# Building fp32 weights from doubles by shifts and masks instead of exponent and mantissa arithmetic, in a fused convolution and SoLU layer

## The chip, the cores and the metric

The kernel runs on one core of a Trainium2 chip. A core has TensorE (PE, matrix products, with its weight loads shown as PEld), VectorE (DVE), ScalarE (ACT), GpSimd (POOL) and SyncE (SP, which issues the DMAs here). Each engine works its own instructions in order and waits for the others by semaphores. The metric is device time in microseconds.

## The reference

A causal convolution over seven taps, one set of softmaxed taps for each of 8 heads, is followed by a two-layer block with a SoLU and a layer norm between the products. Cut to what matters:

```python
# x (8, 4160, 192) f32; weight (8, 7); w_in (192, 1024) f64; w_out (1024, 192) f64; g_ln (1024,)
w = softmax(weight, axis=-1)                     # with 1e-9 in the denominator
x = causal_conv(x, w)                            # each head has 24 of the 192 columns
x = x.reshape(8 * 4160, 192)
h = x @ w_in
e = exp(h - max(h))
solu = h * e / (sum(e) + 1e-9)
mu, var = mean(solu), mean((solu - mu) ** 2)
ln = (solu - mu) / sqrt(var + 1e-6) * g_ln
out = (ln @ w_out).astype(float32)
```

w_in and w_out arrive as doubles, that is as pairs of 32-bit words, and the chip has no double. The kernel makes fp32 values of them itself.

## The kernel before, in words

The 33280 rows of x are 260 tiles of 128 rows. For each tile PE forms ph (128 x 1024) from the convolved input yT and the weights w_in; DVE takes the maximum (`emit_max`), ACT the exponential (`emit_exp`), DVE the product (`emit_mul`), ACT a half-precision copy (`emit_hi`), POOL the rest of it (`emit_lo`); a DMA transposes both, and PE forms the output tile po from them and w_out (`emit_out`). The convolution of the next chunk of rows is done on PE in between (`pc`). The order of the instructions on every engine is the order in which the code is written; nothing is rescheduled.

All weights are held as two halves in fp16, an upper part (whi for w_in, ohi for w_out) and a lower one (wlo, olo), after a scale by a power of two (t_in, t_out). All of that is prepared once at the start, while the first tiles already run. w_in has 192 rows: 128 of them fill A, in two halves of 512 columns (`halves[0]`, `halves[1]`), and the other 64 rows, folded to 128 x 512, are Z. w_out is W, 128 x 1536.

The class `Words` makes floats of the doubles: `exponents` and `mantissas` cut them out of the upper word on DVE, `join` adds the lower word, ACT turns the exponent bits into a power (`powers`), `signs` puts the sign in, and `value` multiplies. For W part of this runs on POOL (`lows`, `whole`, `value`) and on ACT (`floats`, and `out_powers`, which brings g_ln in). ACT's `squares` give the sums from which the scales t_in and t_out come. `settle` makes the lower halves of the first convolved rows and issues their transposes. `out_mean` takes the mean of w_out's columns on PE, `out_upper` subtracts it on DVE and makes ohi on ACT, `out_lower` makes olo on DVE. `first_two` and `second_two` are the code of the first four tiles, in which W's steps are mixed. In `second_two` the order on PE is: two tiles of ph, the first convolution of chunk 1 (`hold`), the sum for t_out, the mean, and then the next tiles.

PSUM holds three pairs of banks for ph and two single banks. A tile's pair comes free with its `emit_mul`; `hold` takes the pair of tile 1, and the sixth tile's ph the pair of the fourth.

Of the kernel before, what the change touches and what calls it, by code (L numbers as in the profile page):

```python
# [8 lines left out]
F16 = mybir.dt.float16  # L9
F32 = mybir.dt.float32  # L10
# [9 lines left out]
def kernel(  # L20
# [10 lines left out]
    P = 128  # L31
# [355 lines left out]
    for j in range(2):  # L387
# [10 lines left out]
    rebias = cp.tile([P, 1], F32, name="rebias")  # L398
    pool.memset(rebias, -916.0 * 2.0**23)
    act.activation(rebias[0:1], rebias[0:1], AF.Copy)  # L400
    mhalf = cp.tile([P, 1], F32, name="mhalf")
    pool.memset(mhalf, -0.5)
    band = cp.tile([TJ, H, TB, K], F32, name="band")
    pool.memset(band, 1.0)
# [14 lines left out]
    even = cp.tile([P, P], F32, name="even")  # L419
    pool.memset(even, 1.0 / F)  # L420
# [6 lines left out]
    class Words:  # L427


        def __init__(self, raw, name):  # L430
            self.name = name
            n = raw.shape[1]
            self.low, self.high = raw.bitcast(U32)[..., 0], raw[..., 1]
            self.n, self.e = n, None
# [4 lines left out]
        def exponents(self, c):  # L439
            if self.e is None:  # L440
                self.e, self.m = (
                    sp.tile(
                        [P, GMAX * D], I32, name=f"{q}_{self.name}", tag="g_raw", bufs=3
                    )[:, 0 : self.n]
                    for q in "em"
                )
            dve.tensor_scalar(
                self.e[:, c], self.high[:, c], 0x7FF00000, None, ALU.bitwise_and
            )

        def mantissas(self, c):
            dve.tensor_scalar(
                self.m[:, c], self.high[:, c], 0xFFFFF, 0x100000,
                ALU.bitwise_and, ALU.bitwise_or,
            )

        def lows(self, c, scale):
            pool.tensor_scalar(
                self.low[:, c].bitcast(F32), self.low[:, c], scale, 1.0,
                ALU.mult, ALU.mult,  # L460
            )

        def floats(self, c):
            act.copy(self.m[:, c].bitcast(F32), self.m[:, c])

        def squares(self, c, to):

            junk = sp.tile([P, F], F32, name=f"oj_{self.name}_{c.start}", tag="sq", bufs=1)
            junk = junk.bitcast(F16)[:, 0 : c.stop - c.start]
            act.activation(  # L470
                junk, self.e[:, c].bitcast(F32), AF.Square, scale=2.0**20, accum_out=to
            )

        def whole(self, c):
            pool.tensor_tensor(
                self.f[:, c], self.m[:, c].bitcast(F32),
                self.low[:, c].bitcast(F32), ALU.add,
            )

        def join(self, c):  # L480
            dve.scalar_tensor_tensor(
                self.f[:, c], self.low[:, c], 2.0**-32, self.m[:, c],
                ALU.mult, ALU.add,
            )

        def powers(self, c):
            act.activation(self.e[:, c], self.e[:, c], AF.Relu, bias=rebias, scale=8.0)

        def signs(self, c, to):
            dve.scalar_tensor_tensor(  # L490
                to[:, c], self.high[:, c], -(2**31), self.e[:, c],
                ALU.bitwise_and, ALU.bitwise_or,
            )

        def value(self, c, powers, eng):
            f = self.f[:, c]
            eng.tensor_tensor(f, f, powers[:, c].bitcast(F32), ALU.mult)

    wi, A, Z = Words(raw_in, "in"), slice(0, F), slice(F, 3 * F // 2)
    HF = F // 2  # L500
    halves = [slice(0, HF), slice(HF, F)]

    def words(c):
        wi.exponents(c)
        wi.mantissas(c)
        wi.join(c)

    def valued(c):

        wi.signs(c, wi.m)  # L510
        wi.value(c, wi.m, dve)
# [23 lines left out]

    words(halves[0])
    wi.powers(halves[0])
    valued(halves[0])
# [11 lines left out]

    tp = pair(0, "tps")
# [16 lines left out]
    words(halves[1])  # L568
    for h in c0.halves(1):
        c0.sum_squares(*h)  # L570
    wi.powers(halves[1])
# [15 lines left out]
    isq = cp.tile([P, 2], F32, name="isq")  # L587
# [15 lines left out]
    going = convolve(*spans0[0], [pq[:, 0:512], pq[:, 512:F]])  # L603
    got0 = [next(going)]
    c0.add_up()
    got0 += going
    wi.squares(A, isq[:, 0:1])
    wi.signs(halves[1], wi.m)
    wi.exponents(Z)
    wi.powers(Z)  # L610
    for f in chain0[1:-3]:
        f()
    wi.squares(Z, isq[:, 1:2])
    for pc, hg in got0:
        c0.upper(pc, *hg)
    wi.value(halves[1], wi.m, dve)
    wi.mantissas(Z)
    c0.open(0, None)
    got1 = got0
    wo, W = Words(raw_out, "out"), slice(0, NFC * D)  # L620

    tp = total(isq, "wi")
    got0 = list(convolve(*spans0[1], [single("pr_0"), single("pr_1")]))
    dve.tensor_reduce(isq[:, 0:1], tp, AX.X, ALU.add)
    for f in root_power(t_in, isq[:, 0:1], 2.0**26, 1e-12):
        f()
    for c in halves:
        act.activation(whi[:, 0, c], wi.f[:, c], AF.Copy, scale=t_in)
# [44 lines left out]
    gate = cp.tile([1, 1], F32, name="gate")  # L673
    o_inv = cp.tile([P, 1], F32, name="o_inv")
    t_out = cp.tile([P, 1], F32, name="t_out")
    osq = cp.tile([P, 1], F32, name="osq")
    wof = wo.f.rearrange("p (c d) -> p c d", d=D)
    mean = None

    def out_powers():  # L680


        woe = wo.e.bitcast(F32).rearrange("p (c d) -> p c d", d=D)
        for j in range(NFC):
# [23 lines left out]
    def out_upper():  # L708
        for c in quarters:
            dve.scalar_tensor_tensor(  # L710
                wof[:, c], wof[:, c], 1.0,
                mean[:, 0:D].unsqueeze(1).broadcast_to([P, NFC // 2, D]),
                ALU.mult, ALU.subtract,
            )
            act.activation(ohi[:, c, :], wof[:, c], AF.Copy, scale=t_out)
# [433 lines left out]
    def first_two():  # L1149
# [21 lines left out]
        wo.value(W, wo.e, pool)  # L1171
# [426 lines left out]
```

## Time and profile before

| | us |
|---|---|
| median of 3 timed runs | 1166.07 |
| lowest and highest | 1162.34, 1166.71 |
| span of the profiled execution, first to last instruction | 1161.5 |
| PE busy in it | 1132.2 |
| DVE busy in it | 1016.8 |
| ACT busy in it | 998.0 |
| POOL busy in it | 878.6 |

The profiled execution shows no other time of its own than its span, which lies 4.6 us under the median of the timed runs and 0.8 us under the lowest of them. Busy time is a sum over the whole span. What the start of the kernel costs has to be read from that stretch.

### The profile page before, as it was taken

The page shows a single profiled execution, that of the slowest core. Times are in us where ns is not written, and L with a number is a line of the kernel's source. Part 1 is how long each engine was busy: PE and PEld are TensorE (multiplying, and loading weights), DVE is VectorE, ACT ScalarE, POOL GpSimd, SP SyncE. Part 2 cuts the span into 40 slices and gives each one's busy share as a digit, 9 for nine tenths or more (in the row PEclk, how much of TensorE's full clock was granted, in tenths as well). Part 3 has the DMA queues.
Part 4 walks back from the last instruction along what each step waited for, and adds up shares of the span by engine and source line. Part 5 has one row for each costly group of instructions (what it writes and reads, how often), then busy time and mean ns, then how long its engine had stood idle before and what let it go on. Part 6 is the DMA issues. An engine that isn't in the chain of part 4 may idle for free.

```text
span 1161.5 us, 22374 instructions
## 1 busy us (share of the span) xinstructions
PE 1132.2 (97%) x7742; PEld 692.4 (60%) x7742; DVE 1016.8 (88%) x2058; ACT 998.0 (86%) x1775; POOL 878.6 (76%) x686
## 2 busy tenths in 40 slices
PE   5898999999999999999999999999999999999998
PEld 3575566656666665655656666665666566566556
DVE  8888898988989898998889989888898988788787
ACT  6998988888888888888888888898888889888886
POOL 2745879987888588887868888588788858855665
PEclk9999999999999999999999999999999999999999
DMA  8799899999999999999999999999999998999988
GB/s 226 171 181 180 185 218 205 205 201 202 200 213 195 195 186 220 207 189 199 202 198 190 208 209 199 187 202 208 206 204 198 195 193 170 174 177 186 181 163 188
DMA packets 727391, 226.95 MB, mean 195 GB/s; under 512 B 651614, under 2 KB 725870, under 8 KB 727278
## 3 DMA queue, kind: packets, MB, share of 16 engines
q1 hardware_dynamic: 727278, 225.53, 100.2%
q8 instruction: 60, 0.98, 0.3%
q14 instruction: 53, 0.43, 0.1%
HBM read 33.00 MB, written 25.56 MB: 50 GB/s over the span
## 4 chain that ended last, share of the span: by engine, by line
PE 88%; DVE 5%; ACT 2%; DMA 2%; issue 2%; POOL 1%; SPq 0%; DVEq 0%; ACTq 0%; POOLq 0%
PE po L859 40%; PE ph L736 36%; PE pc L281 6%; PE ph L759 5%; DVE e L807 1%; DMA pT<-p 1%; DVE ph L790 1%; DMA raw_in<-in_moe_w_in_dram 1%; ACT e L797 1%; ACT sq L819 0%; DVE raw L869 0%; DVE y L322 0%; POOL p L827 0%; PE mean L701 0%; DVE wlo L647 0%
## 5 line engine op out<-in xcount | busy, mean ns | idle before, releaser
L827 POOL TENSOR_TENSOR p<-e,p 128x1024 f16<-128x1024 f32 x257 | 548.3, 2138 | 219.5 <-ACT p L815 218.0
L859 PE MATMUL po<-ohl,pT 128*128 128x192 f16 (+1 forms) x4264 | 539.8, 283 | 7.8 <-DVE raw L869 5.4
L859 PEld LDWEIGHTS <-pT 128*128 128x128 f16 x4264 | 384.4, 98 | 167.1 <-issue 7.6
L736 PE MATMUL ph<-whi,yT 128*128 128x512 f16 x1548 | 419.1, 380 | 2.7 <-DVE e L807 2.6
L790 DVE TENSOR_SCALAR_CACHE_REDUCE ph<-ph,cv 128x1024 f32<-128x1024 f32 x248 | 319.1, 1288 | 72.9 <-PE ph L759 56.6
L797 ACT ACTIVATE e<-ph,sm 128x1024 f32<-128x1024 f32 x260 | 289.4, 1113 | 102.0 <-DVE ph L790 95.8
L807 DVE SCALAR_TENSOR_TENSOR e<-ph,cv,e 128x1024 f32<-128x1024 f32 x248 | 317.1, 1279 | 26.0 <-ACT e L797 25.7
L736 PEld LDWEIGHTS <-yT 128*128 128x128 f16 x2064 | 192.6, 98 | 231.3 <-issue 36.3
L815 ACT CAST p<-e 128x1024 f16<-128x1024 f32 x257 | 266.8, 1039 | 27.9 <-DVE e L807 27.3
L819 ACT ACTIVATE sq<-e 128x1024 f32<-128x1024 f32 x260 | 273.4, 1052 | 0.2
L736 PE MATMUL ph<-wlo,yT 128*128 128x512 f16 x516 | 153.5, 379 | 0.0
L869 DVE TENSOR_REDUCE raw<-po 128x192 f32<-128x384 f32 x247 | 136.3, 552 | 14.3 <-PE po L859 13.9
L243 POOL TENSOR_TENSOR xs<-xr,xs 128x960 f16<-128x960 f32 (+1 forms) x56 | 107.6, 1922 | 1.4
L313 ACT ACTIVATE y<-pc 112x432 f16<-112x432 f32 (+5 forms) x140 | 62.8, 469 | 13.8 <-PE pc L281 8.1
L759 PE MATMUL ph<-wlo,yT 64*128 64x512 f16 x269 | 74.0, 380 | 0.0
L322 DVE SCALAR_TENSOR_TENSOR y<-pc,y 112x432 f16<-112x432 f32 (+5 forms) x140 | 72.2, 532 | 0.8 <-ACT y L313 0.8
L281 PE MATMUL pc<-xs,taps_hi 128*112 128x240 f16 (+1 forms) x448 | 72.9, 261 | 0.0
L759 PE MATMUL ph<-wlo,y 64*128 64x512 f16 x251 | 68.6, 380 | 0.0
L181 DVE TENSOR_REDUCE xa<-xr 128x1 f32<-128x384 f32 x112 | 66.6, 617 | 0.0
L281 PEld LDWEIGHTS <-taps_hi 128*112 128x112 f16 x448 | 52.4, 130 | 16.4
L240 POOL TENSOR_SCALAR xr<-xr,s 128x960 f32<-128x960 f32 (+1 forms) x56 | 57.5, 1027 | 2.9
L281 PE MATMUL pc<-xs,taps_lo 128*112 128x240 f16 (+1 forms) x224 | 58.5, 261 | 0.0
(148 smaller groups left out, 787.6 us busy)
## 6 DMA issues: line engine op xcount, KB each, us to landing
out_dram<-raw SPq DMA_DIRECT2D x127, 192.0 KB, 3.0
xr<-in_x_dram SPq DMA_DIRECT2D x41, 480.0 KB, 4.7
xr<-in_x_dram SPq DMA_DIRECT2D x22, 384.0 KB, 4.1
pT<-p SPq DMA_TRANSPOSE x263, 4.6
y<-yT SPq DMA_DIRECT2D x15, 140.0 KB, 3.1
y<-yT SPq DMA_DIRECT2D x15, 126.0 KB, 3.1
yT<-y SPq DMA_TRANSPOSE x102, 3.7
raw_out<-in_moe_w_out_dram SPq DMA_DIRECT2D x1, 1536.0 KB
```

The lines of the kernel that those rows point to most:

```text
L243: (2.1 * size + 0.2, lambda: pool.tensor_tensor(xl, r, h, ALU.subtract)),
L281: nc.tensor.matmul(o, tp[:, h + j, :], r, start=q == 0, stop=q == len(ops) - 1)
L736: nc.tensor.matmul(bank, lhs, w[:, r, n * 512 : (n + 1) * 512], start=start and j == 0, stop=stop and j == len(ops) - 1,)
L759: nc.tensor.matmul(banks_of(t)[n], y[q, t.off : t.off + P], wlo[q, 1, n * 512 : (n + 1) * 512], start=start, stop=not start,)
L790: dve.tensor_scalar(t.ph, t.ph, t.cv[:, 0:1], None, ALU.mult, ALU.min, accum_out=t.bias)
L797: act.activation(t.e, t.ph, AF.Exp, bias=t.bias, scale=-1.0, accum_out=grp.z[:, g : g + 1])
L807: dve.scalar_tensor_tensor(t.e, t.ph, t.cv[:, 3:4], t.e, ALU.mult, ALU.mult, accum_out=t.grp.s1[:, t.g : t.g + 1],)
L815: act.copy(t.p16[:, :, 0, :], t.halves)
L819: act.activation(junk, t.e, AF.Square, accum_out=t.grp.s2[:, t.g : t.g + 1])
L827: eng.tensor_tensor(t.p16[:, :, 1, :], t.halves, t.p16[:, :, 0, :], ALU.subtract)
L859: nc.tensor.matmul(t.po[:, 0:n], t.pT[:, a, :], w, start=j == 0, stop=j == len(ops) - 1)
L869: dve.tensor_reduce(t.grp.raw[:, t.g, :], t.po[:, 0 : 2 * D].rearrange("p (a d) -> p d a", a=2), AX.X, ALU.add,)
```

## The change

`Words` now builds the float out of the double's bits. `sizes` takes the absolute value of the upper word (on DVE for the two halves of A, on ACT for Z and W), `bounded` raises it to at least 2^-15 (on DVE, with the largest value of each partition as a by-product, for w_in; on POOL for W), `shifted` shifts it by three bits and masks, `signs` puts sign and top exponent bit in, `lows` adds the top three bits of the lower word. Powers, joins and products go. The scale t_in comes from the largest value of each partition, rounded in the same way and summed over partitions by PE. g_ln no longer multiplies W on ACT: it is the weight of the product that makes the mean (`even`), and `out_upper` multiplies by it, in eight pieces of 192 columns instead of two of 768. The squares of W are taken from the float itself, scaled by the largest g_ln of the partition (`most`). The load of g_ln goes ahead of the load of w_out, and that load now waits for a one-element copy on POOL, which waits for the second part of w_in. The diff, cut to its core:

```diff
-    nc.sync.dma_start(
-        raw_out.rearrange("p (c d) t -> p c (d t)", d=D),
-        w_out.rearrange("(c p) d -> p c d", p=P),
-    )
+    nc.sync.dma_start(gl, g_ln.rearrange("(c p) -> p c", p=P))
...
-    pool.memset(band, 1.0)
+    dve.memset(band, 1.0)
...
-    even = cp.tile([P, P], F32, name="even")
-    pool.memset(even, 1.0 / F)
+    pool.tensor_copy(raw_out[0:1, 0, 0:1], raw_in[0:1, F - 1, 0:1])
+    nc.sync.dma_start(
+        raw_out.rearrange("p (c d) t -> p c (d t)", d=D),
+        w_out.rearrange("(c p) d -> p c d", p=P),
+    )
...
+        def sizes(self, c, eng):
+            if eng is act:
+                act.activation(self.m[:, c], self.high[:, c].bitcast(F32), AF.Abs)
+            else:
+                dve.tensor_scalar(
+                    self.m[:, c].bitcast(U32), self.high[:, c], 0x7FFFFFFF, None,
+                    ALU.bitwise_and,
+                )
+        def bounded(self, c, peak=None):
+            m = self.m[:, c]
+            if peak is None:
+                pool.tensor_scalar(m, m, LEAST, 1.0, ALU.max, ALU.mult)
+            else:
+                dve.tensor_scalar(m, m, LEAST, None, ALU.max, ALU.max, accum_out=peak)
+        def shifted(self, c):
             dve.tensor_scalar(
...
+                self.bits[:, c], self.m[:, c].bitcast(U32), 3, 0x3FFFFFF8,
+                ALU.logical_shift_left, ALU.bitwise_and,
+            )
+        def signs(self, c):
+            dve.scalar_tensor_tensor(
+                self.bits[:, c], self.high[:, c], 0xC0000000, self.bits[:, c],
                 ALU.bitwise_and, ALU.bitwise_or,
             )
...
+        def lows(self, c):
             dve.scalar_tensor_tensor(
...
+                self.bits[:, c], self.low[:, c], 29, self.bits[:, c],
+                ALU.logical_shift_right, ALU.bitwise_or,
+            )
...
+    wi.sizes(halves[0], dve)
+    wi.bounded(halves[0], peaks[:, 0:1])
     words(halves[0])
-    wi.powers(halves[0])
-    valued(halves[0])
...
-    words(halves[1])
-    for h in c0.halves(1):
-        c0.sum_squares(*h)
-    wi.powers(halves[1])
+    wi.sizes(halves[1], dve)
+    wi.bounded(halves[1], peaks[:, 1:2])
+    wi.sizes(Z, act)
...
+    act.activation(whi[:, 0, halves[0]], wi.f[:, halves[0]], AF.Copy, scale=t_in)
     settle(*spans0[0], got1)
+    wi.signs(halves[1])
+    wi.lows(halves[1])
+    act.activation(whi[:, 0, halves[1]], wi.f[:, halves[1]], AF.Copy, scale=t_in)
     for j in range(chunks[1].np):
         chunks[1].load(j)
-    nc.sync.dma_start(gl, g_ln.rearrange("(c p) -> p c", p=P))
-    wo.lows(W, 2.0**-32)
-    wi.join(Z)
-    valued(Z)
+    wo.sizes(W, act)
+    wo.bounded(W)
+    words(Z)
...
-    wo.exponents(W)
+    wo.shifted(W)
     for f in chain0[-3:]:
         f()
-    wo.mantissas(W)
...
-    wo.powers(W)
-    wo.floats(W)
...
                 start=(c == 0), stop=(c == NFC - 1),
...
     def out_upper():
-        for c in quarters:
-            dve.scalar_tensor_tensor(
-                wof[:, c], wof[:, c], 1.0,
-                mean[:, 0:D].unsqueeze(1).broadcast_to([P, NFC // 2, D]),
-                ALU.mult, ALU.subtract,
-            )
-            act.activation(ohi[:, c, :], wof[:, c], AF.Copy, scale=t_out)
+        for q in quarters:
+            for c in range(q.start, q.stop):
+                dve.scalar_tensor_tensor(
+                    wof[:, c], wof[:, c], gl[:, c : c + 1], mean[:, 0:D],
+                    ALU.mult, ALU.subtract,
+                )
+            act.activation(ohi[:, q, :], wof[:, q], AF.Copy, scale=t_out)
...
         emit_max(t)
         emit_exp(t)
-        wo.signs(W, wo.e)
-
-        pool.tensor_copy(gate, wo.e.bitcast(F32)[0:1, 0:1])
-        wo.whole(W)
+        wo.signs(W)
         emit_mul(t)
-        out_powers()
+        emit_hi(t)
         emit_max(u)
         emit_exp(u)
-        wo.squares(W, osq)
-        emit_hi(t)
+        wo.lows(W)
+        out_squares()
         settle_rest()
         emit_mul(u)
         emit_hi(u)
...
-        wo.value(W, wo.e, pool)
```

In the order of DVE's instructions the first place is that from the scale of chunk 0 (s) to the lower halves of w_in. Before, with e, m and f the exponents, the integer and the float of w_in, isq the sums of squares and y the convolved rows:

```order
L112 TENSOR_SCALAR s_167<-s_167 128x1
L497 TENSOR_TENSOR f_in<-f_in,m_in 128x512
L452 TENSOR_SCALAR m_in<-raw_in 128x512
L624 TENSOR_REDUCE isq<-pt_wi 128x1
...
L322 SCALAR_TENSOR_TENSOR y_0_0_192<-pq,s_167,y_0_0_192 112x5x64
L481 SCALAR_TENSOR_TENSOR f_in<-raw_in,m_in 128x512
L490 SCALAR_TENSOR_TENSOR m_in<-raw_in,e_in 128x512
L497 TENSOR_TENSOR f_in<-f_in,m_in 128x512
L647 SCALAR_TENSOR_TENSOR wlo<-f_in,t_in,whi 128x512 x2
```

Now, with m the sizes and peaks the largest of each partition:

```order
L112 TENSOR_SCALAR s_163<-s_163 128x1
L456 TENSOR_SCALAR m_in,peaks<-m_in 128x512
L588 TENSOR_SCALAR peak<-peaks 128x3
L591 SCALAR_TENSOR_TENSOR peak<-peaks,peak 128x3
L459 TENSOR_SCALAR f_in<-m_in 128x512
L596 TENSOR_REDUCE t_in<-pt_wi 128x1
...
L322 SCALAR_TENSOR_TENSOR y_0_0_181<-pq,s_163,y_0_0_181 112x5x64
L465 SCALAR_TENSOR_TENSOR f_in<-raw_in,f_in 128x512
L471 SCALAR_TENSOR_TENSOR f_in<-raw_in,f_in 128x512
L459 TENSOR_SCALAR f_in<-m_in 128x512
```

The second half of A got its float ahead of the scale; now its last two steps stand behind the three steps of `settle` (L322), ahead of Z's three.

On ACT the same stretch, from the upper halves of w_in's A to the first exponential, was this before (whi are the upper halves, those of 64x512 belong to Z; pr and y belong to the second half of the first convolved rows):

```order
L628 ACTIVATE whi<-f_in,t_in 128x512 x2
L313 ACTIVATE y_0_0_192<-pr_202,s_167 112x5x96
L313 ACTIVATE y_0_0_192<-pr_203,s_167 112x5x32
L313 ACTIVATE y_0_0_192<-pr_203,s_167 112x5x64
L644 ACTIVATE whi<-f_in,t_in 64x512 x4
L487 ACTIVATE e_out<-e_out,rebias 128x1536
L464 CAST m_out<-m_out 128x1536
L797 ACTIVATE e_297,z_268<-ph_273,sm_295 128x1024
```

The same stretch now:

```order
L605 ACTIVATE whi<-f_in,t_in 128x512
L609 ACTIVATE whi<-f_in,t_in 128x512
L443 ACTIVATE m_out<-raw_out 128x1536
L313 ACTIVATE y_0_0_181<-pr_198,s_163 112x5x96
L313 ACTIVATE y_0_0_181<-pr_199,s_163 112x5x32
L313 ACTIVATE y_0_0_181<-pr_199,s_163 112x5x64
L623 ACTIVATE whi<-f_in,t_in 64x512 x4
L776 ACTIVATE e_286,z_257<-ph_262,sm_284 128x1024
```

Two instructions over W behind Z's upper halves went, and one came ahead of them.

On DVE the next place is that of W's steps around the first two tiles, before (e_out is W's exponents, e_297 and e_313 the tiles'):

```order
L647 SCALAR_TENSOR_TENSOR wlo<-f_in,t_in,whi 64x512 x2
L447 TENSOR_SCALAR e_out<-raw_out 128x1536
L205 TENSOR_SCALAR cv_168<-s_167,t_in 128x1
L117 TENSOR_SCALAR cv_168<-cv_168 128x1
L452 TENSOR_SCALAR m_out<-raw_out 128x1536
L790 TENSOR_SCALAR ph_273,sm_295<-ph_273,cv_168 128x1024
L490 SCALAR_TENSOR_TENSOR e_out<-raw_out,e_out 128x1536
L807 SCALAR_TENSOR_TENSOR e_297,s_0_269<-ph_273,cv_168,e_297 128x1024
L790 TENSOR_SCALAR ph_274,sm_311<-ph_274,cv_168 128x1024
L322 SCALAR_TENSOR_TENSOR y_0_0_192<-pr_202,s_167,y_0_0_192 112x5x96
...
L807 SCALAR_TENSOR_TENSOR e_313,s_0_269<-ph_274,cv_168,e_313 128x1024
```

And now:

```order
L626 SCALAR_TENSOR_TENSOR wlo<-f_in,t_in,whi 64x512 x2
L459 TENSOR_SCALAR f_out<-m_out 128x1536
L205 TENSOR_SCALAR cv_164<-s_163,t_in 128x1
L117 TENSOR_SCALAR cv_164<-cv_164 128x1
L769 TENSOR_SCALAR ph_262,sm_284<-ph_262,cv_164 128x1024
L465 SCALAR_TENSOR_TENSOR f_out<-raw_out,f_out 128x1536
L786 SCALAR_TENSOR_TENSOR e_286,s_0_258<-ph_262,cv_164,e_286 128x1024
L769 TENSOR_SCALAR ph_263,sm_292<-ph_263,cv_164 128x1024
L471 SCALAR_TENSOR_TENSOR f_out<-raw_out,f_out 128x1536
L661 TENSOR_REDUCE most<-gl 128x1
L322 SCALAR_TENSOR_TENSOR y_0_0_181<-pr_198,s_163,y_0_0_181 112x5x96
...
L786 SCALAR_TENSOR_TENSOR e_294,s_0_258<-ph_263,cv_164,e_294 128x1024
```

One step over W's 1536 columns (L452) went from ahead of the first maximum, and one (L471) came between the second tile's maximum and its product, with a reduction of eight columns (L661). Behind the first four tiles every engine has the same instructions in the same order in both kernels.

## Rows read from the trace of the kernel before

**Rows 1.** The page: span and instructions.

```profile
span 1161.5 us, 22374 instructions
```

**Rows 2.** Busy us of each engine (instructions), granted PE clock, DMA, by stretches.

```profile
20.00:30.00 10.00, 6.88 (x27) 2.03 (x26) 9.75 (x14) 7.84 (x11) 2.40 (x5) 1.00 0.95 248
50.00:1161.50 1111.50, 1099.51 (x7556) 670.85 (x7554) 974.68 (x1976) 958.06 (x1703) 855.40 (x663) 1.00 1.01 195
```

**Rows 3.** The chain that ended last, 0 to 60 us: start, us, what.

```profile
32.72 1.76 issue
34.48 2.98 PE pc L281 x16
...
37.69 3.16 PE mean L701 x16
...
40.95 1.82 DVE f_out L710 x2
...
44.03 1.90 PE ph L736 x8
```

**Rows 4.** Timeline of ACT: start, us, instruction, idle time before it.

```profile
14.85 0.63 ACT L470 ACTIVATE oj_in<-e_in 128x512 f16<-128x512 f32 x1
15.48 1.34 ACT L313 ACTIVATE y<-pq,s 112x480 f16<-112x480 f32 x3
17.00 1.34 ACT L628 ACTIVATE whi<-f_in,t_in 128x512 f16<-128x512 f32 x2 [0.17 <-DVE t_in L112]
21.02 2.94 ACT L644 ACTIVATE whi<-f_in,t_in 64x512 f16<-64x512 f32 x4 [1.44 <-DVE f_in L497]
24.78 1.58 ACT L487 ACTIVATE e_out<-e_out,rebias 128x1536 int32<-128x1536 int32 x1 [0.81 <-DVE e_out L447]
```

**Rows 5.** Timeline of DVE, 11 to 20 us.

```profile
11.43 0.43 DVE L447 TENSOR_SCALAR e_in<-raw_in 128x512 int32<-128x512 int32 x1 [0.56 <-DMA raw_in<-in_moe_w_in_dram]
...
13.03 0.69 DVE L490 SCALAR_TENSOR_TENSOR m_in<-raw_in,e_in 128x512 int32<-128x512 int32 x1
13.64 0.42 DVE L447 TENSOR_SCALAR e_in<-raw_in 128x512 int32<-128x512 int32 x1
...
14.73 0.15 DVE L112 TENSOR_SCALAR s<-s 128x1 int32<-128x1 int32 x1
...
16.81 0.15 DVE L112 TENSOR_SCALAR t_in<-t_in 128x1 int32<-128x1 int32 x1
16.88 1.46 DVE L322 SCALAR_TENSOR_TENSOR y<-pq,s,y 112x480 f16<-112x480 f32 x3
```

**Rows 6.** Instructions of line L940, a DVE maximum with a by-product, 192 columns.

```profile
L940 DVE TENSOR_SCALAR_CACHE_REDUCE raw<-raw,t x128: 384/404/411, 96.4 to 1156.0; 128x192 f32<-128x192 f32 x128
```

**Rows 7.** Timeline of PE: the first convolution, in two parts, and the second.

```profile
10.63 1.94 PE L281 MATMUL pq<-xr,taps 128*112 128x120 f32 x8 [1.07 <-ACT taps L563]
...
15.87 1.87 PE L281 MATMUL pr<-xr,taps 128*112 128x120 f32 x16
```

**Rows 8.** Timeline of POOL: its first step over w_out.

```profile
17.42 1.59 POOL L458 TENSOR_SCALAR raw_out<-raw_out 128x1536 f32<-128x1536 uint32 x1 [12.56 <-DMA raw_out<-in_moe_w_out_dram]
```

**Rows 9.** Timeline of DVE, 23 to 37 us.

```profile
23.78 0.96 DVE L447 TENSOR_SCALAR e_out<-raw_out 128x1536 int32<-128x1536 int32 x1
...
25.84 1.30 DVE L790 TENSOR_SCALAR_CACHE_REDUCE ph<-ph,cv 128x1024 f32<-128x1024 f32 x1
...
27.04 1.77 DVE L490 SCALAR_TENSOR_TENSOR e_out<-raw_out,e_out 128x1536 int32<-128x1536 int32 x1
...
33.09 1.28 DVE L807 SCALAR_TENSOR_TENSOR e<-ph,cv,e 128x1024 f32<-128x1024 f32 x1 [0.28 <-ACT e L797]
```

**Rows 10.** DVE groups by form, 0 to 60 us: a product over 160 columns of PSUM.

```profile
L322 DVE SCALAR_TENSOR_TENSOR y<-pc,s,y 112x160 f16<-112x160 f32 x1 | 0.4, 375 | 0.0
```

**Rows 11.** By stretches, as rows 2: the granted PE clock behind the pause.

```profile
35.00:38.50 3.50, 3.50 (x19) 3.50 (x18) 2.63 (x9) 3.50 (x7) 3.50 (x3) 0.51 0.54 113
```

**Rows 12.** What PE waited for from 44 to 130 us: in total, times, longest.

```profile
PE po L859 <- DVE raw L869: 4.8, 4, 1.8
```

More of the change, by code (lines that the diff above doesn't have):

```diff
@@ L430, in __init__ @@
         def __init__(self, raw, name):
-            self.name = name
             n = raw.shape[1]
-            self.low, self.high = raw.bitcast(U32)[..., 0], raw[..., 1]
-            self.n, self.e = n, None
+            self.low, self.high = (raw.bitcast(U32)[..., j] for j in range(2))
+            self.m = sp.tile(
+                [P, GMAX * D], F32, name=f"m_{name}", tag="g_raw", bufs=3
+            )[:, 0:n]
             self.f = xp.tile(
@@ L437, in __init__ @@
             )[:, 0:n]
[L439 to L445, printed above, removed]
-                )
+            self.bits = self.f.bitcast(U32)
+        def sizes(self, c, eng):
[5 more added lines that the diff above has]
+                    ALU.bitwise_and,
+                )
@@ L466, in squares @@
[L466 to L471, printed above, removed]
-            )
[L474 to L478, printed above, removed]
@@ L501 @@
     halves = [slice(0, HF), slice(HF, F)]
+    peaks = cp.tile([P, 3], F32, name="peaks")
+    peak = cp.tile([P, 3], F32, name="peak")
     def words(c):
[L504 to L511, printed above, removed]
+        wi.shifted(c)
+        wi.signs(c)
+        wi.lows(c)
     wtop = cp.tile([TJ, H], F32, name="wtop")
@@ L549, in of_blocks @@
         return t[:, :, a * TB : z * TB].rearrange("p h (q c) -> p q h c", c=TB)
+    for h in c0.halves(1):
+        c0.sum_squares(*h)
     tp = pair(0, "tps")
@@ L602 @@
     pq = pair(1, "pq")
[L603 to L610, printed above, removed]
+    c0.add_up(single("pt_x0"))
+    got1 = list(convolve(*spans0[0], [pq[:, 0:512], pq[:, 512:F]]))
     for f in chain0[1:-3]:
         f()
-    wi.squares(Z, isq[:, 1:2])
-    for pc, hg in got0:
+    for pc, hg in got1:
         c0.upper(pc, *hg)
-    wi.value(halves[1], wi.m, dve)
-    wi.mantissas(Z)
+    wi.bounded(Z, peaks[:, 2:3])
+    pbits, kbits = peak.bitcast(U32), peaks.bitcast(U32)
+    dve.tensor_scalar(
+        pbits, kbits, 3, 0x3FFFFFF8, ALU.logical_shift_left, ALU.bitwise_and
+    )
+    dve.scalar_tensor_tensor(
+        pbits, kbits, 0xC0000000, pbits, ALU.bitwise_and, ALU.bitwise_or
+    )
+    tp = total(peak, "wi")
+    wi.shifted(halves[1])
+    dve.tensor_reduce(t_in, tp, AX.X, ALU.add)
+    dve.tensor_scalar(t_in, t_in, 1e-6, 2.0**-13, ALU.max, ALU.mult)
+    dve.tensor_scalar(
+        t_in.bitcast(I32), t_in.bitcast(I32), EXPO, None, ALU.bitwise_and
+    )
+    inverse_power(t_in, t_in, 1)
     c0.open(0, None)
-    got1 = got0
     wo, W = Words(raw_out, "out"), slice(0, NFC * D)
-    tp = total(isq, "wi")
     got0 = list(convolve(*spans0[1], [single("pr_0"), single("pr_1")]))
[L624 to L628, printed above, removed]
+    act.activation(whi[:, 0, halves[0]], wi.f[:, halves[0]], AF.Copy, scale=t_in)
     settle(*spans0[0], got1)
+    wi.signs(halves[1])
+    wi.lows(halves[1])
+    act.activation(whi[:, 0, halves[1]], wi.f[:, halves[1]], AF.Copy, scale=t_in)
     for j in range(chunks[1].np):
         chunks[1].load(j)
-    nc.sync.dma_start(gl, g_ln.rearrange("(c p) -> p c", p=P))
-    wo.lows(W, 2.0**-32)
-    wi.join(Z)
-    valued(Z)
+    wo.sizes(W, act)
+    wo.bounded(W)
+    words(Z)
     for pc, hg in got0:
```

52 lines of the change are left out of this document (14 added, 38 removed).

## The prediction

> **What bounds the kernel now.** The span is 1161.5 us [rows 1], and the stretches come next: from 50 us on PE is busy 1099.5 of 1111.5 us, while between 20 and 30 us it works only 6.9 of 10 and DVE works 9.75 [rows 2]. So the body is bound by PE, the start is not, and what delays PE's last long stop at the start is added to the end. The chain of waits says where that stop is [rows 3]: PE pauses 1.76 us ahead of the first convolution of chunk 1 (34.48), runs that and the mean, DVE subtracts the mean (40.95), and PE goes on at 44.03, from where its work is gapless for a long time. The timelines of ACT and DVE then tell what stands ahead of 34.48. Everything that the change touches lies ahead of 44.03, and behind the first four tiles the order is the same. I therefore carry times of single events from the trace into the new order and look at two of them: the start of the convolution (34.48) and PE's restart (44.03).
>
> **The change part by part.**
>
> *The scale t_in.* The second half of w_in lands at 11.43 [rows 5]. On it DVE now does sizes (0.43, as L447) and bounded. The trace has no maximum with a by-product over 512 columns: the same kind over 192 takes 0.40 [rows 6], and over 1024 columns of PSUM 1.30 [rows 9], so 1.08 ns a column between them and 0.40 + 320 x 1.08 ns = 0.75, which I take; below it lies L447's 0.43, above it two streams and a read of the by-product, 0.69 + 0.15. Then the five small steps to s (0.19 each, 0.15 and a gap): 13.6 instead of 14.88. ACT's sizes of Z (0.63 as L470, [rows 4]) start when Z is there, at 13.6 at the latest [rows 5]; bounded on DVE 14.2 to 15.0, two steps over three columns to 15.35. Before, it took 16.96 - 15.48 = 1.5 us from the end of the squares to t_in, with five small steps; now four are left: 1.3, so t_in is there at 16.6, some 0.35 earlier. The convolution now runs in one piece of 16 passes at the slow rate of that stretch (8 in 1.94, [rows 7]): 10.8 to 14.7, so ACT's first upper halves start at 14.7 instead of 15.48, ahead of t_in either way. Early on, then, a gain of 0.35.
>
> *Upper halves of w_in.* Before, both halves of A were ready at t_in and ACT rounded them at once (17.00 to 18.34). Now DVE first does the three steps of settle (1.46, to 18.05) and then signs and lows of the second half, 0.69 each by L490 [rows 5]: 19.45. Behind that wait on ACT stand: the second half's upper part (0.65), W's sizes (1.5, L487's 1.58 less what overlaps), the three upper halves of the second convolved part (1.34), and Z's four (2.94) [rows 4]. That gives 20.1, 21.6, 22.95 and 25.9, where Z's were done at 23.96 before: +1.9. PE needs them for the last four products of the first tile (0.24 each by rows 3, so 1.0): ph is there at 26.9.
>
> *W's load* is issued when the second part of w_in has landed: 11.43, a copy (0.2), an issue (0.6). Before, it landed at 17.42, 6.0 us behind that part [rows 8, 5], with Z's bytes still in front of it. So 18.2 if it takes the same 6.0 behind its issue. ACT takes it up at 20.1. The cover is thus 1.9 us, a third of the load's own time, and what is beyond it goes one for one into Z's upper halves. The load of g_ln costs nothing: only the convolved rows' transposes and W stand behind it.
>
> *W's steps on DVE.* The first maximum was at 25.84 behind DVE's own steps over W; now at 26.95, when ph is there: +1.1. Of the 1.9, the 0.8 is what the removed mantissas (of L447's kind and size, 0.96) leave free. Signs over 1536 columns stand behind it as before (L490's 1.77, [rows 9]). Between the second tile's maximum and its product lows is new: 1.77 by the same row, since it also reads two streams; at least 0.96, L447's time for one stream. I take 1.77, as two streams go at 1.05 ns a column (0.69 for 512, 1.77 for 1536) where one goes at half of that (0.43 and 0.96). The largest g_ln adds 0.15. DVE waited 0.28 for the exponential there [rows 9], which is now hidden. So the product of the second tile starts 1.1 + 1.77 + 0.15 - 0.28 - 0.1 = 2.6 later, at 35.7, and the convolution behind it on PE at 37.05.
>
> *From there to the mean* PE's work is the same 16 + 2 + 16 passes: 6.35 us from 34.48 to 40.85, 3.5 of it at half clock (granted 0.51, 1.2 GHz, [rows 11]) behind the pause. Taken over as it is: 43.4. What ACT and POOL lose (powers, g_ln, joins, products) was not waited for: POOL's float of W was there before PE came to the mean.
>
> *Subtracting the mean* in eight pieces of 192 columns instead of two of 768 (1.82 together, [rows 3]). A piece of 160 columns of PSUM takes 0.375 [rows 10]; back to back some 0.05 of it overlaps, so 0.33 to 0.40 each, 2.6 to 3.2: +0.8 to +1.4, taken as +0.9. The fourth tile's product stands behind it on DVE, and PE's restart behind that.
>
> *Sum:* 2.6 + 0.9 = +3.5 us. PE restarts at 47.5; the span becomes 1165.0, and on the median of the runs, which lies 4.6 above the span, 1169.6. The bounds: the half clock (next part) takes 1.7 off or adds 2.9, W's load adds up to 1.1, lows takes 0.8 off.
>
> **The rivals.**
>
> *The clock.* PE's pause ahead of the convolution grows from 1.76 to 3.3 us, since the fourth tile's ph ends some 1.1 later and the convolution 2.6. Before, the granted clock fell behind the shorter pause and was up again 3.5 us later. Three ways: it falls as before (my sum). It does not fall in this stretch: 3.5 us at 0.51 lose 1.7, so the sum is +1.8, 1167.9; the pauses of the start were of 1 to 2 us before and only this one shows a fall, so it hangs on little. Or it is low over the whole stretch, having fallen in the pause itself: 6.35 - 1.7 = 4.65 at full rate, 9.3 at half, +2.9, so the sum is +6.4, 1172.5. For the last speaks that the pause is nearly twice as long; against it, that before the low stretch began only 0.5 us behind the convolution's start and ended under full work. The Trainium skill (TensorE: Matmul & The Clock Gate, HAM oscillation) says that work behind an idle stretch runs throttled, so that a pause is paid twice; by it alone the third way would be the likeliest. The trace agrees that the clock falls behind a pause (0.51 in 35.0 to 38.5).
>
> *W's load comes late.* If it took half as long again, 9.0 us, it would land at 21.2 and ACT would wait 1.1: +4.6, 1170.7. For it: it is issued only when the second part of w_in is there. Against it: of Z's bytes, which lay in front of it, less is left by then.
>
> *Stops of the body vanish* (the other side). From 44 to 130 us PE still waits 4.8 us in four places for DVE's taking up of po [rows 12], in a stretch where the start's backlog is worked off. POOL and ACT come out of the start with less behind them, so those tiles' transposes can come earlier. From 3.5 us of these 4.8 on the change is no loss; with all of them gone it is -1.3, 1164.8. Against it: those waits hang on DVE, ACT and DMA orders that have not changed and that are shifted by the same start.
>
> **How the numbers follow.** My sum 0.50; clock not fallen 0.16; clock low throughout 0.12; late load 0.07; stops vanish 0.10; something else 0.05. The timed runs of one kernel spread by 4.4 us, so that 0.5%, 5.8 us, is about what a measurement here can tell from no change. All but the low clock lie within it: slower 0.11, faster 0.05, same 0.84. The range takes in the vanished stops and the low clock with a microsecond of the runs' own spread: 1163.5 to 1173.0.
>
> **What would show it.** In the changed kernel's trace: t_in's last step ending near 16.6; Z's last upper half near 25.9 and directly in front of it on ACT W's sizes and three upper halves without a wait for W's load; the first maximum near 26.95; lows of 1.77 between the second maximum and its product; the convolution of chunk 1 near 37.0; eight pieces of 0.33 to 0.40; PE's restart near 47.5; the stretch from there to the end as long as before. The prediction is wrong if signs or lows run at two columns a cycle, if ACT's wait at Z is not there, or if PE's busy time behind 50 us is not what sets the end.

## The result, and the profile after

The changed kernel takes 1169.38 us (median of 8 runs, 1166.57 to 1172.38), the kernel before 1163.53 us (8 runs, 1161.68 to 1166.71): ratio 1.0048, 95% interval 1.0035 to 1.0061. It became 5.9 us slower. The profiled execution has a span of 1169.0 us instead of 1161.5 [rows 1], with a time of its own of 1171.04, which is 1.7 above the median of its runs.

The same windows as [rows 2] first (busy us of each engine with its instructions, granted clock, DMA):

```profile
20.00:30.00 10.00, 5.78 (x18) 1.45 (x17) 9.59 (x9) 5.17 (x8) 6.11 (x5) 0.83 0.98 286
50.00:1169.00 1119.00, 1107.39 (x7603) 676.12 (x7601) 978.66 (x1983) 963.18 (x1714) 858.64 (x664) 1.00 1.02 194
```

From 20 to 30 us PE does 1.1 us less than before and its granted clock is 0.83 instead of 1.00. From 50 us on it is busy all but 11.6 us (12.0 before): the body is bound by PE in both kernels. The chain of waits, as in [rows 3]:

```profile
20.67 5.25 DVE wlo L626 x2
25.96 2.00 PE ph L728 x5
...
28.96 1.35 DVE ph L769 x2
...
35.63 3.12 issue
38.74 2.37 PE pc L281 x16
...
41.35 3.77 PE mean L680 x16
...
45.14 2.69 DVE f_out L690 x8
...
49.09 2.56 PE ph L715 x8
```

PE restarts at 49.09 instead of 44.03: +5.1, where 47.5 was predicted. The row that the prediction did not have is the first one: making the lower half (wlo) of A's second 512 columns, otherwise a step of 0.75 us, holds the chain for 4.7 us. On ACT (as in [rows 4]) things went as foreseen, and somewhat sooner:

```profile
15.94 0.73 ACT L605 ACTIVATE whi<-f_in,t_in 128x512 f16<-128x512 f32 x1
18.92 0.72 ACT L609 ACTIVATE whi<-f_in,t_in 128x512 f16<-128x512 f32 x1 [2.25 <-DVE f_in L471]
19.54 1.62 ACT L443 ACTIVATE m_out<-raw_out 128x1536 f32<-128x1536 f32 x1
21.07 1.34 ACT L313 ACTIVATE y<-pr,s 112x480 f16<-112x480 f32 x3
22.30 2.93 ACT L623 ACTIVATE whi<-f_in,t_in 64x512 f16<-64x512 f32 x4
```

Z's last upper half ends at 25.2 (predicted 25.9), with W's sizes and the three upper halves ahead of it, and nothing there waits for W's load. Now POOL's timeline, the durations of wlo's steps before (L647) and after (L626; ns, min/median/max), and PE's wait:

```profile
21.26 5.41 POOL L454 TENSOR_SCALAR m_out<-m_out 128x1536 f32<-128x1536 f32 x1 [10.01 <-ACT m_out L443]
```

```profile
L647 DVE SCALAR_TENSOR_TENSOR wlo<-f_in,t_in,whi x4: 735/745/750, 20.9 to 23.0; 128x512 f16<-128x512 f32 x2, 64x512 f16<-64x512 f32 x2
```

```profile
L626 DVE SCALAR_TENSOR_TENSOR wlo<-f_in,t_in,whi x4: 733/747/4655, 20.6 to 26.6; 128x512 f16<-128x512 f32 x2, 64x512 f16<-64x512 f32 x2
```

```profile
PE ph L728 <- DVE wlo L626: 4.2, 1, 4.2
```

Before, all four lower halves take 0.75 us. After, three do and one takes 4.66, and that one falls into POOL's new step, which raises W's sizes (`bounded`): 5.41 us for 128x1536, where POOL's old step of the same size took 1.59 [rows 8]. PE stands still for 4.2 us for it. The steps over W on DVE, behind the first and the second maximum, as in [rows 9]:

```profile
30.17 1.75 DVE L465 SCALAR_TENSOR_TENSOR f_out<-raw_out,f_out 128x1536 uint32<-128x1536 uint32 x1
...
34.25 1.75 DVE L471 SCALAR_TENSOR_TENSOR f_out<-raw_out,f_out 128x1536 uint32<-128x1536 uint32 x1
...
35.92 0.15 DVE L661 TENSOR_REDUCE most<-gl 128x1 f32<-128x8 f32 x1
```

Last, the granted clock. Before, one stretch of about 3.4 us at half, 1.2 of 2.4 GHz [rows 11]. After, there are four:

```profile
26.00:29.50 3.50, 3.50 (x9) 0.71 (x8) 3.09 (x6) 0.00 (x0) 1.37 (x5) 0.54 1.10 328
39.75:43.25 3.50, 3.50 (x17) 3.50 (x16) 3.24 (x10) 3.19 (x6) 2.13 (x1) 0.53 0.48 105
50.00:53.50 3.50, 3.50 (x14) 1.39 (x13) 3.21 (x6) 3.41 (x10) 2.69 (x1) 0.53 1.08 202
97.75:101.25 3.50, 3.07 (x13) 1.93 (x13) 3.09 (x6) 2.14 (x5) 2.52 (x3) 0.53 0.76 143
```

The first three lie behind PE's waits of 4.2, 3.1 and 1.7 us. The third and fourth lie behind the restart, where PE has no slack. The fourth begins in a stop of 1.8 us in the body (96.38 to 98.18), and the kernel before has the same stop, at 90.17 to 91.97, and runs on at full clock. PE's timeline, before and after (the same 16 products of an output tile take 2.12 us and 3.67):

```profile
91.97 2.12 PE L859 MATMUL po<-ohl,pT 128*128 128x384 f16 x16 [1.80 <-DVE raw L869]
```

```profile
98.18 3.67 PE L838 MATMUL po<-ohl,pT 128*128 128x384 f16 x16 [1.80 <-DVE raw L848]
```

The start of each tile's maximum on DVE, minus that of the same tile before, shows what that cost: +4.3 us at the fourth tile, +5.1 at the fifth, +6.2 at the ninth (behind 50.0 to 53.5), +7.8 at the fifteenth (behind 97.75 to 101.25), +7.8 still at the hundred-and-first, and +7.3 at the last.

### The profile page after: what moved, and what is told of

Read it like the earlier page. It is cut to its first block, busy times and chain, and to the rows that moved or that the text cites. A ratio compares the mean times of both kernels' runs of the same rounds, so it can differ in the third digit from the quotient of the medians.

```text
span 1169.0 us, 22356 instructions
## 1 busy us (share of the span) xinstructions
PE 1137.2 (97%) x7742; PEld 694.8 (59%) x7742; DVE 1022.5 (87%) x2069; ACT 991.3 (85%) x1760; POOL 876.6 (75%) x682
## 4 chain that ended last, share of the span: by engine, by line
PE 90%; DVE 5%; ACT 2%; issue 2%; DMA 1%; SPq 0%; POOL 0%; ACTq 0%; DVEq 0%
PE po L838 41%; PE ph L715 37%; PE pc L281 6%; PE ph L738 6%; DVE e L786 1%; DVE ph L769 1%; DMA pT<-p 1%; ACT e L776 1%; ACT sq L798 1%; DMA xr<-in_x_dram 1%; DVE wlo L626 0%; DVE raw L848 0%; DVE y L322 0%; PE mean L680 0%; ACT y L313 0%
## 5 line engine op out<-in xcount | busy, mean ns | idle before, releaser
L786 DVE SCALAR_TENSOR_TENSOR e<-ph,cv,e 128x1024 f32<-128x1024 f32 x248 | 316.8, 1278 | 25.2 <-ACT e L776 25.0
L322 DVE SCALAR_TENSOR_TENSOR y<-pc,y 112x432 f16<-112x432 f32 (+5 forms) x140 | 72.1, 531 | 0.9 <-ACT y L313 0.9
```

The lines of the kernel that those rows point to most:

```text
L786: dve.scalar_tensor_tensor(t.e, t.ph, t.cv[:, 3:4], t.e, ALU.mult, ALU.mult, accum_out=t.grp.s1[:, t.g : t.g + 1],)
```

## The experiments

The theory (theory 1 in the expectations) is that POOL's step is slow by itself, that it locks DVE's step with two inputs out meanwhile, and that PE's longer stops bring half clock onto the path. Its rivals: the two engines slow each other (theory 2); wlo is slow for another reason (theory 3); the loss is all in lows and the eight pieces.

**Measured by themselves, at the end of the program.**

```diff
+    for f in (largest, product):      # POOL, 128x1536: (max, mult); (mult, mult)
+        for g in (lambda: None, single_in, beside):   # DVE: none; 1 input x2; 2 inputs x2
+            apart(); f(); g()
```

> The changed kernel with the raising of W's sizes moved to VectorE, and behind the last tile six measured steps: GpSimd's largest-of step (max, mult) and a plain product (mult, mult), 128x1536 fp32 each, once alone, once beside two VectorE steps with one SBUF input (128x512) and once beside two with two SBUF inputs. Theory 1 (the step itself is slow on GpSimd, and VectorE's two-input step is held up behind it): the largest-of step takes 4 to 5.5 us alone and in all three settings, the product 1.6 us; VectorE's two-input step beside the largest-of step takes over 3 us, its one-input step 0.4 us. Theory 2 (the two engines slow each other): alone both take about 1.6 us, and the largest-of step comes to 4 us or more only beside the two-input steps. Theory 3 (neither; wlo was slow for another reason): all take about 1.6 us, VectorE's 0.4 and 0.7 us.

POOL's timeline (L1569 the largest-of step, alone, beside one-input and beside two-input steps; L1572 the product in the same order), then DVE's of the same stretch:

```profile
1171.32 5.39 POOL L1569 TENSOR_SCALAR ma<-ma 128x1536 f32<-128x1536 f32 x1 [3.69 <-DVE ma L1556]
...
1177.21 5.60 POOL L1569 TENSOR_SCALAR ma<-ma 128x1536 f32<-128x1536 f32 x1 [0.27 <-DVE ma L1556]
...
1183.38 5.87 POOL L1569 TENSOR_SCALAR ma<-ma 128x1536 f32<-128x1536 f32 x1 [0.26 <-DVE ma L1556]
...
1189.76 1.48 POOL L1572 TENSOR_SCALAR ma<-ma 128x1536 f32<-128x1536 f32 x1 [0.26 <-DVE ma L1556]
...
1194.02 1.97 POOL L1572 TENSOR_SCALAR ma<-ma 128x1536 f32<-128x1536 f32 x1 [0.26 <-DVE ma L1556]
```

```profile
1177.16 5.94 DVE L1566 TENSOR_SCALAR mb<-mb 128x512 f32<-128x512 f32 x2
...
1183.33 5.16 DVE L1560 SCALAR_TENSOR_TENSOR mb<-mb,mc 128x512 f32<-128x512 f32 x2
...
1193.96 2.56 DVE L1560 SCALAR_TENSOR_TENSOR mb<-mb,mc 128x512 f32<-128x512 f32 x2
```

Alone, the largest-of step takes 5.39 us and the product 1.48: theory 1, as far as POOL goes. DVE's pair of two-input steps (0.69 each at the shortest) takes 5.16 us beside the one and 2.56 beside the other. Against the expectation the one-input steps (0.43 at the shortest) are held too, 5.94 us for two: the first, started 0.05 us ahead of POOL, takes 0.43, the second 5.59.

**Without the step, with a product in its place, and on DVE.**

```diff
     wo.sizes(W, act)
-    wo.bounded(W)
```

> The changed kernel without the raising of W's sizes on GpSimd (left out of the computation). Theories 1 and 2: the second lower half of w_in takes 0.75 us instead of 4.66, the first maximum comes at about 27.0 instead of 28.96, the convolution of chunk 1 at 36.8 instead of 38.74, and TensorE's restart at 47.1 instead of 49.09; the time falls by about 2 us to 1167.4, and by up to 1.7 more if the half clock of 49.9 to 53.3 goes with it. Theory 3: the second lower half stays over 4 us and the time stays at 1169.4.

```diff
-                pool.tensor_scalar(m, m, LEAST, 1.0, ALU.max, ALU.mult)
+                pool.tensor_scalar(m, m, 1.0, 1.0, ALU.mult, ALU.mult)
```

> The changed kernel with GpSimd's step on W's sizes as a product by one (mult, mult) in the same place and of the same size (the raising is left out of the computation). Theory 1: the step takes 1.6 us, the second lower half of w_in at most 2.4, the first maximum comes at 27 to 27.5, and the time is that of the kernel without the step, 1167.4 or less. Theory 2: the step still takes over 4 us and the lower half with it, and the time stays near 1169.4.

```diff
-    wo.bounded(W)                      # behind wo.sizes(W, act)
...
-                pool.tensor_scalar(m, m, LEAST, 1.0, ALU.max, ALU.mult)
+                dve.tensor_scalar(m, m, LEAST, 1.0, ALU.max, ALU.mult)
...
+    wo.bounded(W)
     wo.shifted(W)
```

> The changed kernel with the raising of W's sizes on VectorE, directly ahead of the shift of W (128x1536, expected 0.96 us). Theories 1 and 2: the lower halves of w_in take 0.75 us each, the added 0.96 us lies ahead of a first maximum that still waits for its products until about 27.0, so the restart of TensorE is at about 47.1 and the time falls by 2 us to 1167.4 or a little lower, as without the step. Rival: VectorE becomes the bound ahead of the first maximum and the gain is only 1 us. Theory 3: no gain, or 1 us more.

All runs stand in the table below. Without the step the time is 1167.04, with the product 1167.10: 2.3 us less than with the largest-of step, or 1.7 to 1.8 if each is taken against the kernel before as timed together with it (+4.1 and +4.2 instead of +5.9). With the product, POOL's step in its place and the four lower halves are:

```profile
21.06 2.06 POOL L454 TENSOR_SCALAR m_out<-m_out 128x1536 f32<-128x1536 f32 x1 [10.54 <-ACT m_out L443]
```

```profile
L626 DVE SCALAR_TENSOR_TENSOR wlo<-f_in,t_in,whi x4: 743/747/802, 20.4 to 23.7; 128x512 f16<-128x512 f32 x2, 64x512 f16<-64x512 f32 x2
```

So a POOL step on as many columns is free in that place, and this one is not. On DVE it costs 0.96 us ahead of a first maximum that then waits for DVE (1168.28, its rival's case). The intervals of the timed runs overlap, those of the changed kernel and of these three; the stage up to the first maximum, in the table, tells them apart.

**ScalarE's order, then settle behind the second product** (each on top of the kernel ahead of it).

```diff
+    for pc, hg in got0:
+        c0.upper(pc, *hg)
     settle(*spans0[0], got1)
...
     words(Z)
-    for pc, hg in got0:
-        c0.upper(pc, *hg)
```

> The changed kernel with the raising of W's sizes on VectorE and the three upper halves of the second convolved part (1.34 us on ScalarE) ahead of the second half of w_in's A, in ScalarE's wait of 2.25 us there. If ScalarE's order (W's sizes and those three ahead of Z's uppers) is the second term of the loss, Z's uppers end 1.3 us earlier, VectorE goes on without its wait of 1.0 us at Z's lower halves, the first maximum comes some 1.0 to 1.3 us earlier than with the raising on VectorE alone, and the time falls by 1 to 1.3 us, to 1167.0. Rival: VectorE's own work (raising and shift of W, 1.9 us) is the bound there and the time stays at 1168.

```diff
-        settle_rest()
         emit_mul(u)
         emit_hi(u)
+        settle_rest()
```

> As the kernel before this one in the list, and the three steps of settle (1.46 us on VectorE) behind the second tile's product instead of ahead of it. If the 1.77 us of lows over W between the second maximum and its product delay the convolution of chunk 1 one for one, taking 1.46 us out of the same stretch brings convolution, mean and restart 1.46 us forward, and the time to 1165.5. Rival: the exponential of the second tile or the sum of W's squares is late next, and less than 0.5 us comes of it; or the transposes of the moved part come too late for the fifth tile, and TensorE waits there instead.

1166.73 and 1165.08 us. Both expectations hold in the traces: the stage to the first maximum gets 1.15 us shorter, that from there to the convolution 1.38.

**The fourth tile's product ahead of the subtraction**, on the kernel with settle moved, and on the kernel before.

```diff
-        out_upper()
         numerators(u)
+        out_upper()
         out_lower()
```

> As the kernel before this one in the list, and the product of the fourth tile ahead of the subtraction of the mean on VectorE. If the eight pieces (2.69 us) hold up the fourth tile's product and TensorE's restart, the restart comes right behind the fifth tile, 1.7 us earlier, and the first output tile then waits for the lower half of w_out; net gain 0.7 to 1.7 us, to 1164. Rival: the output tile's wait takes all of it back and the time stays.

> The kernel before, with the product of the fourth tile ahead of the subtraction of the mean, as in the run above. If the restart is what counts, TensorE's wait of 0.93 us at 44.03 goes and the time falls by 0.9 us to 1162. Rival: no difference.

A miss: 1166.51 and 1165.82 us, 1.4 and 2.9 slower than the kernels they came from. In the first the stage to the restart is 1.8 us shorter, and PE then waits 2.0 us for the transposed halves. In the second it restarts at 43.15 instead of 44.03 and waits 0.4 for the lower half of w_out; the span of its profiled execution (1161.3) is no longer than before, so what the median lost is not in that trace and stays open. What became of the gain is there: the lower half of w_out, two steps on DVE, now runs beside POOL's subtractions and takes 3.14 and 3.73 us instead of 1.94. In the second kernel PE then waits another 0.86 for a product (at 51.26), and from the seventh tile to the hundred-and-first it is 0.4 behind the kernel before.

**Two pieces instead of eight, on the kernel with settle moved.**

```diff
-            for c in range(q.start, q.stop):
-                dve.scalar_tensor_tensor(
-                    wof[:, c], wof[:, c], gl[:, c : c + 1], mean[:, 0:D], ...
+            dve.scalar_tensor_tensor(
+                wof[:, q], wof[:, q], 1.0, mean[:, 0:D]...broadcast_to([P, NFC // 2, D]), ...
```

> The kernel with the raising on VectorE, ScalarE's other order and settle behind the second product (1165.1 us), with the mean subtracted in two pieces of 768 columns as before the change (g_ln is left out of the subtraction). The eight pieces took 2.69 us in the traces, two took 1.82. If that difference stands on the path to the restart, the restart comes 0.9 us earlier and the time falls to 1164.2. Rival: a start that is earlier by less than a microsecond is given back in the body, where TensorE then waits longer for the transposed halves, and the time stays at 1165.

1164.54 us, 0.5 less, between the two expectations; the runs can't tell it from either. Nor can the profile price the pieces alone: no half clock falls in it at all, though PE stops for 1.76 us ahead of the convolution as in the kernel it came from. It does say what is late next: with the restart at 42.77 instead of 44.72, the first output tile waits for the transposed halves of its rows. PE's timeline:

```profile
46.81 2.15 PE L838 MATMUL po<-ohl,pT 128*128 128x192 f16 x24 [1.60 <-DMA pT<-p]
```

**Zeros in PE's stops.**

```diff
+    def emit_zeros(t, count):
+        for j in range(count):
+            nc.tensor.matmul(
+                banks_of(t)[j % NH], t.yT[:, 0, t.off : t.off + P],
+                zeros[:, 0:1].broadcast_to([P, 512]), start=False, stop=False,
+            )
```

> The changed kernel with products by zeros (128x512, added to banks of tiles that are being summed, so that results stay) in TensorE's three stops of the start: 19 ahead of the products with w_in's lower half, 14 behind the fourth tile's products, 8 within the fifth tile's, sized by 0.215 us each to the stops of 4.2, 3.1 and 1.7 us. If the granted clock falls because TensorE stood still, the half-clock pieces of 3.4 us that the changed kernel shows (four, against one before) become fewer by two or three, convolution and mean run in 4.7 instead of 6.4 us, no half clock falls on the work behind the restart, and the time falls by 3 to 4 us to 1166. If the clock does not hang on the stops, the pieces stay, and the time stays at 1169.4 or rises by what of the zeros sticks out.

> The kernel with the raising on VectorE, ScalarE's other order and settle behind the second product (1165.1 us), with eight products by zeros in each of the two stops of 1.75 us (ahead of the convolution of chunk 1 and ahead of the restart). If the clock hangs on the stops: no half clock from 35 to 49 us in most executions, time down by 1 to 2 us to 1163.5. Else no change, or up to 0.4 us more.

> The kernel before, with eight products by zeros ahead of its convolution of chunk 1 (a stop of 1.76 us) and four ahead of its restart (0.93 us). If the clock hangs on the stops, its one piece of half clock at 35.0 to 38.45 goes and the time falls by 1.5 to 1.7 us, to 1161.4; else it stays at 1163.

In the profiles the clock did as expected: there is no half clock in the start or the body of any of the three. In the changed kernel with zeros:

```profile
39.75:43.25 3.50, 3.42 (x26) 2.41 (x25) 3.50 (x7) 2.32 (x4) 1.69 (x2) 1.00 0.45 87
50.00:53.50 3.50, 3.50 (x26) 2.03 (x25) 3.47 (x7) 3.41 (x8) 2.60 (x1) 1.00 1.13 211
97.75:101.25 3.50, 3.50 (x24) 2.15 (x24) 3.17 (x6) 2.14 (x4) 2.15 (x2) 1.00 0.90 168
```

Its tiles' shift against before goes from +5.5 at the first maximum to +5.8 at the fifth and +5.9 at the hundred-and-first (+4.0 at the last), where the changed kernel's went from +3.1 to +7.8. The mean granted clock of the timed runs rose from 0.9942 to 0.9987 in the changed kernel and from 0.9977 to 0.9992 in that with settle moved; in the kernel before it is 0.9982 with zeros and without. The times did not follow: 1168.13, 1168.59, 1166.37, where 1166, 1163.5 and 1161.4 were expected. The traces show three things against them; whether the other runs had them too is not shown. First, x landed late in the profiles of the first two. ACT's timeline in the changed kernel, then in the same with zeros:

```profile
8.77 0.52 ACT L187 ACTIVATE xj<-xr 128x384 f32<-128x384 f32 x1 [1.92 <-DMA xr<-in_x_dram]
```

```profile
11.48 0.52 ACT L187 ACTIVATE xj<-xr 128x384 f32<-128x384 f32 x1 [4.85 <-DMA xr<-in_x_dram]
```

Second, in the kernel with settle moved PE comes to its last eight zeros only behind a new wait of 1.1 us (at 42.23), so that they get onto the path, and its stage to the restart is 9.9. Third, in the kernel before with zeros the tiles run 1.7 to 1.8 us ahead from the fifth to the forty-first, and are 0.9 late at the two-hundred-and-first: PE waits 4.4 us in five places of the body for the transposed halves, where it waited 1.7 in one before. PE's waits in it from 130 to 1150 us:

```profile
PE po L870 <- DMA pT<-p: 4.4, 5, 1.7
```

**All of it in one table.** Times in us, with the ratio to the kernel before as timed together with it; then from the profile the start of the first convolution (pq), and how long from there to the first maximum, to the convolution of chunk 1, and to the restart.

| kernel | time | ratio, 95% interval | pq | to max | to conv | to restart |
|---|---|---|---|---|---|---|
| before | 1163.53 | | 10.63 | 15.2 | 8.6 | 9.6 |
| changed | 1169.38 | 1.0048 [1.0035, 1.0061] | 11.11 | 17.9 | 9.8 | 10.4 |
| no step on POOL | 1167.04 | 1.0034 [1.0022, 1.0045] | 11.84 | 15.3 | 9.8 | 10.3 |
| product on POOL | 1167.10 | 1.0033 [1.0024, 1.0043] | 10.90 | 15.4 | 9.8 | 10.4 |
| on DVE | 1168.28 | 1.0037 [1.0026, 1.0048] | 11.73 | 16.0 | 9.8 | 8.7 |
| + ACT's order | 1166.73 | 1.0032 [1.0019, 1.0045] | 11.19 | 14.8 | 9.8 | 10.1 |
| + settle later | 1165.08 | 1.0020 [1.0010, 1.0030] | 11.14 | 14.8 | 8.4 | 10.4 |
| + two pieces | 1164.54 | 1.0012 [1.0003, 1.0022] | 10.90 | 14.8 | 8.4 | 8.6 |
| settle later, product first | 1166.51 | 1.0032 [1.0020, 1.0043] | 12.22 | 14.8 | 8.4 | 8.6 |
| before, product first | 1165.82 | 1.0018 [1.0006, 1.0030] | 10.63 | 15.4 | 8.6 | 8.6 |
| changed, zeros | 1168.13 | 1.0039 [1.0026, 1.0051] | 13.82 | 17.5 | 9.8 | 8.7 |
| settle later, zeros | 1168.59 | 1.0046 [1.0034, 1.0058] | 13.20 | 14.8 | 8.4 | 9.9 |
| before, zeros | 1166.37 | 1.0030 [1.0018, 1.0042] | 10.66 | 14.8 | 8.6 | 7.9 |

No version beats the kernel before, whose median was 1162.8 to 1163.5 each time. "To restart" is 1.7 shorter where no half clock falls on convolution and mean (on DVE, and with zeros in the changed kernel). With two pieces none falls there either, and of the 1.8 some 0.9 can be the pieces (1.81 us instead of 2.69).

## Why the prediction was right in its number and wrong in its sum

The time lies in the range and near the figure, 1169.4 against 1169.6, and the loss is of the sign foretold. But the loss was 5.9 us and not 3.5, and that the figure came so close is luck: two errors cancelled. The two largest terms of the loss, POOL's step and the half clock behind the restart, stood in no rival; they belong to "something else", which had 0.05. I set the time 4.6 us over the span, as the median of three runs, 1166.07, stood to the profiled span; each run's own span lies only some 2 us under its time (1171.04 and 1169.0), and more runs of before gave 1163 to 1163.5. From 1161.5 with 3.5 and 1.9 the sum comes to 1166.9, 2.5 under the measured time.

- *"The first maximum ... now at 26.95, when ph is there: +1.1."* This step failed: 28.96, +3.1. I followed ACT and DVE, which were right to a microsecond, and gave POOL's new step over W no price at all, neither its own nor that of the steps beside it. Without it the stage is 15.3 us instead of 17.9, and before it was 15.2: of the +1.1 that I had worked out from ACT's queue only 0.1 is there; t_in came 0.7 sooner than in my sum. The Trainium skill (SBUF — State Buffer, "Who interferes with whom") says that VectorE and GpSimd share a pair of ports as an exclusive lock, taken by whoever starts first for its whole instruction, and that two SBUF inputs, or a form that uses both ports, put a VectorE step on it. The trace agrees as to the hold: 0.75 becomes 4.66 beside a POOL step that takes 5.39 alone. It does not show the hold to last the whole instruction, since the held step ends 0.8 us before POOL's record does.
- *t_in* was there at 15.9, 0.7 sooner than predicted, with bounded at 0.69 and a read of 0.08, near the 0.75 worked out. ACT's queue at Z did what was said, and 25.2 instead of 25.9 follows from t_in.
- *W's load* did not show; the rival of a late load is out.
- *lows*: 1.75 and 0.15 measured for 1.77 and 0.15; the stage from maximum to convolution grew by 1.1 (predicted +1.5). Right in the steps, 0.4 too much for the stage.
- *Eight pieces*: 2.69 for 2.6 to 3.2, +0.87. Right in size. What they cost at the end is open: with two pieces the time is 0.5 less, which the runs can't tell from nothing or from 0.9.
- *The clock.* Convolution and mean ran at half clock as before, 6.4 us, as I took it over. What I missed are the pieces behind the restart: +1.2 at 50.0, +1.6 at 97.75. I had asked what the longer pause does to the stretch behind it, and not to the work after the restart. With zeros in the stops of the start the changed kernel has none of its pieces, and from the first maximum to the hundred-and-first tile only 0.4 us are lost, instead of 4.7; that the first three hang on those stops is borne out by the timed runs too, since three pieces of 3.4 us at half clock are 0.0044 of the mean granted clock, and it rose by 0.0045. The fourth is not explained so: the stop in the body got no zeros, it stands in all fourteen profiles with 1.8 us, and half clock falls there in four of them. A stop does not always bring half clock either: in the kernel with two pieces none followed on stops of 1.1 to 1.8 us.
- *Stops of the body.* They did not vanish: 4.3 us in three places for 4.8 in four [rows 12]. But the reason given against it was too simple: the kernel before with zeros restarts 2.1 us sooner and loses it in the body. What is gained at the start is not passed on one for one.

Not foreseen either: the change puts ACT's sums of chunk 0 ahead of the taps, so the first convolution waits for x. It starts at 10.63 to 10.66 in three profiles of before and its variants, and at 10.90 to 13.82 in the changed kernel and its.

In the profiled execution the +7.5 are: 5.1 up to the restart (0.5 for x, 2.6 to the first maximum, 1.1 to the convolution, 0.8 from there), 2.7 for the two pieces of half clock behind it, less 0.5 later in the body, and a rest of 0.2. The 5.9 of the medians can't be split so, since only this execution has a trace. It also stays open why three kernels that restart sooner than the kernel before by 0.9 to 2.1 us (two pieces; before with the product first; before with zeros) have medians 0.7 to 1.9 us above their profiled executions.

## What to carry to other kernels

Give every moved or new GpSimd step a price of its own, and then ask which VectorE steps run beside it: a step off the chain can stop the chain by holding a VectorE step that is on it. A stop of TensorE costs its length and, in some executions, a half clock behind it (here 3.4 us at a time), which may fall where there is no slack, even behind the restart. Before calling a microsecond at the start a microsecond at the end, look at what waits next; here the transposed halves were that close. And take the base of a forecast from spans and times of the same executions.

## What the runs showed of the hardware that was not expected

- GpSimd's (max, mult) over 128x1536 fp32 takes 5.39 us alone and (mult, mult) 1.48, in the same place and on the same data.
- VectorE's one-input fp32 step from SBUF to SBUF (128x512, 0.43 us) was held to 5.59 us beside the former, longer than a two-input one (0.69 us, held to 4.55).
- In the changed kernel POOL's subtraction over 1024 columns, 2.14 us elsewhere, took 3.70 while VectorE's two-input step over W, started 0.03 us earlier, ran for 1.75: POOL was held there, and so the hold was seen in both directions.
- VectorE's blocked two-input step ended some 0.8 us before the recorded end of POOL's (max, mult) (25.90 and 26.67), in the measured steps too (1188.49 and 1189.25). The one-input step ended 0.3 us behind it (1183.10 and 1182.81), and beside (mult, mult) both ended behind POOL, by 0.3 and 0.5 us. Whether the hold ends earlier or POOL's record is too long was not settled.
